# Held full-row stores, 512-column weight loads, a later place for the state products and a split last eviction in a fused linear-attention and gated-FFN kernel

## The chip, the cores and the metric

The kernel runs on one core of a Trainium2 chip. The metric is the device time of an execution in microseconds (us); on one core that is the time of that core. Each ratio compares the runs of two kernels that ran in the same rounds.

## The reference

Attention with a decaying state over blocks of the sequence, then a gated feed-forward over all tokens:

```python
# q, k, v: (4, 8, 768, 64) float32; lam: (8,); state kv: (64 x 64) per batch and head
intra = (q_b k_b^T * Dmask) v_b                  # within a block of the sequence
inter = (q_b * lam_pow) kv                       # with the state of the earlier blocks
out_b = intra + inter
kv = lam_block * kv + (k_b * rev_pow)^T v_b      # "state product"
# the 4 x 768 = 3072 tokens of 512 features:
y = (sigmoid(x @ w_gate) * (x @ w_val)) @ w_out  # 512 -> 1536 -> 512
```

## The kernel before

The kernel takes the sequence in six blocks of 128 positions (512 tokens with the batch of 4). A block has an attention part, a gate/value phase of twelve tiles (`gv`), and a projection of four token tiles (`po`). A plan lists the units, and the attention of the next block is hung behind units of this one. The order of instructions on each engine is the order of the program.

```python
def load_gv(f0, f1):                       # f0, f1: tiles of 128 columns, f32 -> bf16 on the way
    fs = slice(f0 * 128, f1 * 128)
    nc.gpsimd.dma_start(out=WG[:, :, fs], in_=wg_r[:, :, fs])
    nc.gpsimd.dma_start(out=WV[:, :, fs], in_=wv_r[:, :, fs])

def piece_po(n, tt, c0, c1, eng):          # projection of block n, token tile tt, columns c0 to c1
    ...                                    # 12 matmuls po += HT[n, ft]^T WO[:, ft, c0:c1]
    (eng.copy if eng is nc.scalar else eng.tensor_copy)(o, po[:, :c1 - c0])
    nc.sync.dma_start(out=out[..., c0:c1], in_=o)

# loads, in order, all on the gpsimd queue (cut: k, q, v of block 0; gv 0 to 6)
load_gv(6, 8)
load_gv(8, 10)
load(1, "k", 0, 2)
load(1, "q", 0, 2)
load_gv(10, 12)
load_wo(0, 256)                            # first half of WO's columns
load(1, "k", 2, 4)
load(1, "q", 2, 4)
load_wo(256, 512)                          # second half
load(1, "v")
load(2, "kq")

# block 0 (cut)
behind[5] = [pair(piece_c, 0, 0), pair(piece_c, 0, 1)]   # state products of block 0
behind[8] = [trans(1, 0)]                                # block 1: transposes, scores, masks
behind[9] = [pair(piece_s, 1, 0), m_(1, 0)]
behind[10] = [m_(1, 1)]
for ft in range(NFT):
    gv(0, ft, *behind[ft])
after = {(0, 1): [kd(1, 0)], (0, 2): [trans(1, 1)],
         (0, 3): [pair(piece_s, 1, 1), m_(1, 2), kd(1, 2)], ...}
for j in range(2):                                       # block 0's projection in two halves of
    for tt in range(B):                                  # columns, as WO's second half lands late
        po(0, tt, *after.get((j, tt), []), c=(256 * j, 256 * (j + 1)))
```

From block 2 on, k and q are transposed by DMA on the sync queue, which also issues the stores.

Of the kernel before, what the change touches and what calls it, by code (L numbers as in the profile page):

```python
# [16 lines left out]
def kernel(  # L17
# [11 lines left out]
    nc = tc.nc  # L29

    B, H, S, D = q.shape
    C = 128
    NSTEP = S // C
    HP = H // 2
    DM = H * D
# [35 lines left out]
    def swapped(n, b):  # L71
        return n > 0 and b >= NB2
# [10 lines left out]
    def load(n, what, b0=0, b1=B):  # L83
        sl = slice(n * C, (n + 1) * C)
        for c in what:
            if (c, n) not in T_:
                T_[c, n] = qkv.tile([128, B, H, D], BF16, tag=c + "b", name=c + "b",
                                      bufs=5 if c == "v" else 4)
            src = {"q": q, "k": k, "v": v}[c]
            nat = b1 if n == 0 or c == "v" else min(b1, NB2)  # L90
            if b0 < nat:
                nc.gpsimd.dma_start(  # L92
                    out=T_[c, n][:, b0:nat],
                    in_=src[b0:nat, :, sl, :].rearrange("b h s d -> s (b h) d"))
            if nat < b1:
                m = max(nat, b0)
                for u in range(2):
                    nc.gpsimd.dma_start(  # L98
                        out=T_[c, n][:, m:b1, u::2, :],
                        in_=src[m:b1, 1 - u::2, sl, :].rearrange("b h s d -> s (b h) d"))  # L100

    def load_gv(f0, f1):
# [4 lines that stand above are left out]
    def load_wo(c0, c1):  # L107
        nc.gpsimd.dma_start(out=WO[:, :, c0:c1], in_=wo_r[:, :, c0:c1])
# [110 lines left out]
    def t_(c, n, bs):  # L219
        ps = ps_at.tile([128, len(bs), HP, C], BF16, name="t" + c, tag="ps")  # L220
        for i, b in enumerate(bs):
            for hp in range(HP):
                nc.tensor.transpose(ps[:, i, hp, :], T_[c, n][:, b, 2 * hp:2 * hp + 2, :], ident)
        (tqs if c == "q" else tks)[n, bs[0]] = ps
# [15 lines left out]
    def e_k(n, bs, parts=1):  # L240
        t = trsb.tile([128, 2, HP, C], BF16, tag="KS", name="KS")
        w = len(bs) // parts
        for i in range(parts):
            nc.scalar.copy(t[:, i * w:(i + 1) * w], tks[n, bs[0]][:, i * w:(i + 1) * w])
        for i in range(len(bs)):
            KS[n, bs[i]] = t[:, i]
# [4 lines left out]
    def xbar(n):  # L251
        for c, d in (("k", KT), ("q", QT)):
            d[n] = qtp.tile([128, B, HP, C], BF16, tag=c + "t", name=c + "t")
            nc.sync.dma_start_transpose(
                out=d[n].rearrange("p b hp s -> p (b hp) s"),
                in_=T_[c, n].rearrange("p b h d -> p (b h d)"))
        for b in range(B):
            KS[n, b] = KT[n][:, b]

    def piece_s(n, bs):  # L260
        for b in bs:
            sp = [ps_at.tile([128, HP, C], FP32, name=f"sp{u}", tag="ps") for u in range(2)]
            for hp in range(HP):
                for u in range(2):
                    us = slice(u * 64, (u + 1) * 64)
                    nc.tensor.matmul(sp[u][:, hp, :], lhsT=KS[n, b][us, hp, :],  # L266
                                     rhs=QS[n, b][us, hp, :],
                                     start=(hp == 0), stop=(hp == HP - 1), skip_group_check=True)
            SP[n, b] = sp

    def piece_m(n, b):
        MT[n, b] = mtp.tile([128, 2, HP, C], BF16, tag="MT", name="MT")
        for u in range(2):
            nc.vector.tensor_tensor(out=MT[n, b][:, u], in0=SP[n, b][u],  # L274
                                    in1=(mask if n else mask0)[:, 1 - u if swapped(n, b) else u],
                                    op=ALU.mult)
# [69 lines left out]

    OB = {}

    def piece_po(n, tt, c0, c1, eng):
        if (n, tt) not in OB:  # L350
            OB[n, tt] = osb.tile([128, DM], FP32, tag="ob", name="ob")
        po = ps_ff.tile([128, DM], FP32, name="po", tag="ff")
        for ft in range(NFT):
            nc.tensor.matmul(po[:, :c1 - c0], lhsT=HT[n, ft][:, tt * 128:(tt + 1) * 128],  # L354
                             rhs=WO[:, ft, c0:c1], start=(ft == 0), stop=(ft == NFT - 1))
        o = OB[n, tt][:, c0:c1]
        (eng.copy if eng is nc.scalar else eng.tensor_copy)(o, po[:, :c1 - c0])  # L357
        nc.sync.dma_start(out=out[tt * S + n * C:tt * S + (n + 1) * C, c0:c1], in_=o)



# [2 lines left out]
    def zeros(m):  # L364
        for _ in range(m):
            nc.tensor.matmul(zps, lhsT=Sb[:, 0, 0:2, :], rhs=Sb[:, 0:2], start=True, stop=True)  # L366
# [17 lines left out]
    tables_late()  # L384
    piece_s(0, [0])
    piece_m(0, 0)
    piece_s(0, [1])
    piece_m(0, 1)
    t_("k", 0, [2, 3])
    e_k(0, [2, 3], parts=2)  # L390
    zeros(2)
    t_("q", 0, [2])
    e_q(0, [2], nc.scalar)
# [27 lines left out]
    for n in range(2):  # L421
        make_kd(n)
    load_gv(6, 8)
    load_gv(8, 10)
    load(1, "k", 0, 2)
    load(1, "q", 0, 2)
    load_gv(10, 12)
    load_wo(0, 256)
    load(1, "k", 2, 4)
    load(1, "q", 2, 4)  # L430
# [6 lines left out]
    def gate(n):  # L437
        for i, t in enumerate((KT[n], QT[n])):
            nc.gpsimd.tensor_copy(gates[:, i:i + 1], t[:, B - 1, HP - 1, C - 1:C])  # L439

    def next_loads(n):
        xbar(n)
        gate(n)
        load(n, "v")
        if n + 1 < NSTEP:
            load(n + 1, "kq")
# [5 lines left out]
    def unit(f, *more):  # L452
        plan.append((f, list(more)))

    def gv(n, ft, *more):
        unit(lambda: piece_gv(n, ft), *more)

    def po(n, tt, *more, c=(0, DM), eng=nc.scalar):
        unit(lambda: piece_po(n, tt, *c, eng), *more)

    def pair(f, n, bp):
        return lambda: f(n, [2 * bp, 2 * bp + 1])

    def m_(n, b):
        return lambda: piece_m(n, b)

    def trans(n, bp):
        def go():
            bs = [2 * bp, 2 * bp + 1]
            t_("k", n, bs)  # L470
            e_k(n, bs)
            t_("q", n, bs)
            e_q(n, bs)
        return go

    def att(n):
        def go():
            piece_i(n)
            piece_a(n, range(B))
            piece_x(n, range(B))  # L480
            if n < NSTEP - 1:
                piece_c(n, [0, 1])
                piece_c(n, [2, 3])
        return go

    def kd(n, h0):
        return lambda: piece_kd(n, [h0, h0 + 1])

    behind = {ft: [] for ft in range(NFT)}
# [2 lines left out]
    behind[0].append(swap_halves)  # L492
    behind[1].append(lambda: make_mask(0))
    behind[3].append(lambda: make_mask(1))
    behind[5] = [pair(piece_c, 0, 0), pair(piece_c, 0, 1)]
    behind[8] = [trans(1, 0)]
    behind[9] = [pair(piece_s, 1, 0), m_(1, 0)]
    behind[10] = [m_(1, 1)]
    for ft in range(NFT):
        gv(0, ft, *behind[ft])  # L500
    after = {(0, 1): [kd(1, 0)], (0, 2): [trans(1, 1)], (0, 3): [pair(piece_s, 1, 1), m_(1, 2), kd(1, 2)],
             (1, 0): [m_(1, 3), kd(1, 4)], (1, 1): [kd(1, 6)], (1, 2): [att(1)]}
    for j in range(2):
        for tt in range(B):
            po(0, tt, *after.get((j, tt), []), c=(256 * j, 256 * (j + 1)))
# [1 line left out]
    for n in range(1, NSTEP):  # L507
        nx = n + 1
        more = [[] for i in range(NFT)]
        if nx < NSTEP:  # L510
            more[3] = [lambda nx=nx: e_q(nx, [0, 1])]
            more[4] = [pair(piece_s, nx, 0), m_(nx, 0)]
            more[5] = [m_(nx, 1), lambda nx=nx: e_q(nx, [2, 3])]
            more[7] = [pair(piece_s, nx, 1), m_(nx, 2)]
            more[8] = [m_(nx, 3)]
            more[11] = [att(nx)]
        if nx < NSTEP - 1:
            for i in range(4):
                more[6 + i].append(kd(nx, 2 * i))
            more[5].append(lambda nx=nx: make_kd(nx))  # L520
        if n == 1:
            more[4:11] = more[3:10]
            more[3] = []
            more[2].append(lambda: next_loads(2))
            more[8].append(lambda: next_loads(3))
        for ft in range(NFT):
            gv(n, ft, *more[ft])
        for tt in range(B):
            if n == NSTEP - 1 and tt == B - 1:
                po(n, tt, c=(0, 256))  # L530
                po(n, tt, c=(256, 512), eng=nc.vector)
            else:
                more = [lambda n=n: next_loads(n + 3)] if tt == B - 1 and n + 3 < NSTEP else []
                po(n, tt, *more)
# [35 lines left out]
```

## Time and profile before

Median 229.34 us of 3 runs (229.26 to 229.42).

| what | value | where it is read |
|---|---|---|
| PE busy | 216.2 of 227.6 us, 95% | page |
| DMA engines busy | 90% or more in slices 1 to 10 | page, row DMA |
| PE waits for WO's second half | 1.48 us | PE waits, timeline |
| block to block, PE | 34.6 us | chain |
| last eviction's end to the end of the span | 2.89 us | timeline, last DMA |

In the views, PE is the engine of the matmuls and PEld its weight loads; ACT (scalar) and DVE (vector) copy PE's finished results out, which is called an eviction; POOL (gpsimd) issues the loads, and SPq are instructions of the sync engine, which issues the stores. WG, WV and WO are the gate, value and output weights. On PE, `zps` is a clear at the start, `tk` and `tq` are transposes of k and q, `sp` scores, `cp` state products, `gp` and `vp` the gate/value phase, and `po` the projection. KS is the copy of the transposed k that the scores read.

The page of the kernel before, the busy rows of PE and DMA (tenths, in 40 slices of 5.7 us):

```profile
span 227.6 us, 4227 instructions
PE 216.2 (95%) x1689; PEld 110.9 (49%) x1713; DVE 101.6 (45%) x186; ACT 100.9 (44%) x216; POOL 59.5 (26%) x75
...
PE   6689999979999999999999999999999999999994
...
DMA  7999999999939999995995939012100012100022
```

PE is the bound, but slice 8 of its row (counted from zero; 45.5 to 51.2 us) is not full, and the DMA engines are at least 90% busy until about 62 us, where slice 11 begins. The table of who PE waited for (total us, times, longest):

```profile
PE zps L366 <- DVE Sb L147: 1.5, 1, 1.5
PE po L354 <- DMA WO<-in_moe_w_out_dram: 1.5, 1, 1.5
PE tq L223 <- DMA qb<-in_q_dram: 1.2, 2, 0.7
```

The timeline of PE before (start, length, operation, count; in brackets the idle time ahead of it) shows where the WO wait stands: between block 1's scores (sp) and the second half of the projection (po).

```profile
44.13 1.47 PE L354 MATMUL po<-WO,ht 128*128 128x256 bf16 x12
45.54 0.62 PE L266 MATMUL sp<-QS,KS 64*128 64x128 bf16 x16
47.63 1.58 PE L354 MATMUL po<-WO,ht 128*128 128x256 bf16 x13 [1.48 <-DMA WO<-in_moe_w_out_dram]
```

While WO's second half is on its way, four stores are issued. The DMA view from 40 to 48 us, of the kernel before, gives them 12.3% of the engines' time (q1 carries sync's DMAs; q0, which queues ahead, sums overlapping packets and so passes 100%):

```profile
q0 software_dynamic: 5371, 1.27, 167.5%
q1 hardware_dynamic: 288, 0.26, 12.3%
```

The end of the kernel before: the last 256 columns are evicted by DVE, then stored. The timeline, and the record of the last store alone with its time from issue to landing:

```profile
224.25 0.42 DVE L357 COPY ob<-po 128x256 f32<-128x256 f32 x1 [9.63 <-PE po L354]
```

```profile
L358 SPq DMA_DIRECT2D out_dram<-ob x1: 332/332/332, 224.7 to 224.7; - x1
...
DMA to landing us min/median/max: 1.7/1.7/1.7
```

The eviction ends at 224.68, the store lands at 226.40, and the span ends at 227.57 us.

### The profile page before, as it was taken

The page shows a single profiled execution, that of the slowest core. Times are in us where ns is not written, and L with a number is a line of the kernel's source. Part 1 is how long each engine was busy: PE and PEld are TensorE (multiplying, and loading weights), DVE is VectorE, ACT ScalarE, POOL GpSimd, SP SyncE. Part 2 cuts the span into 40 slices and gives each one's busy share as a digit, 9 for nine tenths or more (in the row PEclk, how much of TensorE's full clock was granted, in tenths as well). Part 3 has the DMA queues.
Part 4 walks back from the last instruction along what each step waited for, and adds up shares of the span by engine and source line. Part 5 has one row for each costly group of instructions (what it writes and reads, how often), then busy time and mean ns, then how long its engine had stood idle before and what let it go on. Part 6 is the DMA issues. An engine that isn't in the chain of part 4 may idle for free.

```text
span 227.6 us, 4227 instructions
## 1 busy us (share of the span) xinstructions
PE 216.2 (95%) x1689; PEld 110.9 (49%) x1713; DVE 101.6 (45%) x186; ACT 100.9 (44%) x216; POOL 59.5 (26%) x75
## 2 busy tenths in 40 slices
PE   6689999979999999999999999999999999999994
PEld 1444454867444644444544444554444544444443
DVE  4754657145468620388430378530368600333300
ACT  5767443565337732338532328532333342333221
POOL 7997654700067009302900030000000000000000
PEclk9999999999999999999999999999999999999998
DMA  7999999999939999995995939012100012100022
GB/s 115 147 174 200 193 180 181 194 193 178 212 57 153 147 209 106 207 193 98 109 157 154 192 53 82 0 49 92 46 3 0 0 49 92 46 0 3 0 94 92
DMA packets 106195, 25.31 MB, mean 111 GB/s; under 512 B 94144, under 2 KB 103744, under 8 KB 106176
## 3 DMA queue, kind: packets, MB, share of 16 engines
q0 software_dynamic: 82816, 13.90, 79.3%
q1 hardware_dynamic: 22896, 11.01, 19.5%
q8 instruction: 13, 0.21, 0.4%
q10 hardware_dynamic: 464, 0.14, 0.3%
q14 instruction: 6, 0.05, 0.1%
HBM read 28.32 MB, written 6.29 MB: 152 GB/s over the span
## 4 chain that ended last, share of the span: by engine, by line
PE 77%; DMA 15%; POOL 5%; issue 2%; DVE 0%; POOLq 0%
PE po L354 25%; PE vp L342 23%; PE gp L336 22%; DMA WO<-in_moe_w_out_dram 7%; DMA qb<-in_q_dram 5%; DMA WG<-in_moe_w_gate_dram 3%; PE op L296 2%; PE sp L266 2%; PE op L285 1%; POOL vb L92 1%; POOL kb L92 1%; PE cp L314 1%; POOL WG L104 1%; POOL qb L92 1%; POOL WV L105 1%
## 5 line engine op out<-in xcount | busy, mean ns | idle before, releaser
L345 DVE TENSOR_TENSOR ht<-sg,vp 128x512 bf16<-128x512 bf16 x72 | 49.4, 686 | 94.3 <-PE vp L342 92.7
L342 PE MATMUL vp<-XT,WV 128*128 128x512 bf16 x287 | 73.8, 379 | 0.3
L336 PE MATMUL gp<-XT,WG 128*128 128x512 bf16 x272 | 71.5, 379 | 1.5 <-issue 0.8
L339 ACT ACTIVATE sg<-gp 128x512 bf16<-128x512 f32 x72 | 43.0, 597 | 66.5 <-PE gp L336 63.0
L354 PE MATMUL po<-WO,ht 128*128 128x512 bf16 (+1 forms) x343 | 63.6, 342 | 1.8 <-DMA WO<-in_moe_w_out_dram 1.5
L354 PEld LDWEIGHTS <-ht 128*128 128x128 bf16 x348 | 33.5, 98 | 29.8 <-issue 1.5
L342 PEld LDWEIGHTS <-WV 128*128 128x128 bf16 x288 | 28.2, 98 | 34.0 <-DMA WV<-in_moe_w_val_dram 0.2
L336 PEld LDWEIGHTS <-WG 128*128 128x128 bf16 x288 | 27.3, 98 | 32.4 <-issue 0.3
L357 ACT COPY ob<-po 128x512 f32<-128x512 f32 (+1 forms) x28 | 14.4, 515 | 45.3 <-PE po L354 45.3
L274 DVE TENSOR_TENSOR MT<-sp,mask 128x512 bf16<-128x512 f32 x48 | 30.5, 682 | 1.9 <-PE sp L266 1.9
L120 ACT ACTIVATE kd<-kb,kds 128x128 bf16<-128x128 bf16 (+1 forms) x72 | 23.8, 402 | 0.0
L439 POOL COPY gates<-kt 128x1 bf16<-128x1 bf16 x4 | 0.7, 186 | 54.8 <-DMA kt<-kb 54.8
L306 ACT CAST XT<-op 128x512 bf16<-128x512 f32 x21 | 10.9, 597 | 5.6 <-PE op L296 5.6
L92 POOL DMA_DIRECT2D vb<-in_v_dram x7 | 10.9, 1563 | 1.4 <-issue 0.9
L323 DVE SCALAR_TENSOR_TENSOR Sb<-Sb,dec,cp 128x128 bf16<-128x128 bf16 x32 | 8.6, 342 | 3.3 <-PE cp L314 3.3
L98 POOL DMA_DIRECT2D kb<-in_k_dram x10 | 8.8, 895 | 3.2 <-DMA WO<-in_moe_w_out_dram 2.3
L98 POOL DMA_DIRECT2D qb<-in_q_dram x10 | 8.9, 918 | 1.3 <-DMA kb<-in_k_dram 0.8
L92 POOL DMA_DIRECT2D qb<-in_q_dram x7 | 8.4, 1205 | 0.8 <-POOLq L554 0.8
L366 PE MATMUL zps<-Sb 128*128 128x512 bf16 x19 | 6.5, 469 | 1.6 <-DVE Sb L147 1.5
L92 POOL DMA_DIRECT2D kb<-in_k_dram x6 | 6.9, 1158 | 1.4 <-DMA WV<-in_moe_w_val_dram 0.8
L296 PE MATMUL op<-MT,vb 128*64 128x128 bf16 x184 | 6.5, 221 | 0.0
L296 PEld LDWEIGHTS <-vb 128*64 128x64 bf16 x184 | 5.3, 110 | 1.3 <-issue 0.4
(55 smaller groups left out, 81.9 us busy)
## 6 DMA issues: line engine op xcount, KB each, us to landing
out_dram<-ob SPq DMA_DIRECT2D x19, 256.0 KB, 2.0
vb<-in_v_dram POOLq DMA_DIRECT2D x5, 512.0 KB, 7.0
qb<-in_q_dram POOLq DMA_DIRECT2D x7, 256.0 KB, 8.3
kb<-in_k_dram POOLq DMA_DIRECT2D x6, 256.0 KB, 8.0
WO<-in_moe_w_out_dram POOLq DMA_DIRECT2D x2, 768.0 KB, 14.6
WG<-in_moe_w_gate_dram POOLq DMA_DIRECT2D x5, 256.0 KB, 9.2
WV<-in_moe_w_val_dram POOLq DMA_DIRECT2D x5, 256.0 KB, 9.8
kb<-in_k_dram POOLq DMA_DIRECT2D x10, 128.0 KB, 8.6
```

Of the source, the lines that this page charges most:

```text
L92: nc.gpsimd.dma_start(out=T_[c, n][:, b0:nat], in_=src[b0:nat, :, sl, :].rearrange("b h s d -> s (b h) d"))
L98: nc.gpsimd.dma_start(out=T_[c, n][:, m:b1, u::2, :], in_=src[m:b1, 1 - u::2, sl, :].rearrange("b h s d -> s (b h) d"))
L120: nc.scalar.mul(KD[n][:, at, i, :], T_["k", n][:, at, i, :], kds[:, h:h + 1])
L274: nc.vector.tensor_tensor(out=MT[n, b][:, u], in0=SP[n, b][u], in1=(mask if n else mask0)[:, 1 - u if swapped(n, b) else u], op=ALU.mult)
L296: nc.tensor.matmul(OP[n, b][rows_of(w), hp, :], lhsT=T_["v", n][:, b, h, :], rhs=MT[n, b][:, slot(n, b, h) % 2, hp, :], start=(n == 0 and ...
L306: (e.tensor_copy if e is nc.vector else e.copy)(XT[n][:, :, b, :], OP[n, b])
L336: nc.tensor.matmul(gp, lhsT=WG[:, mt, fs], rhs=x[:, mt, :], start=(mt == 0), stop=(mt == NMT - 1))
L339: nc.scalar.activation(sg, gp, AF.Sigmoid)
L342: nc.tensor.matmul(vp, lhsT=WV[:, mt, fs], rhs=x[:, mt, :], start=(mt == 0), stop=(mt == NMT - 1))
L345: nc.vector.tensor_mul(HT[n, ft], sg, vp)
L354: nc.tensor.matmul(po[:, :c1 - c0], lhsT=HT[n, ft][:, tt * 128:(tt + 1) * 128], rhs=WO[:, ft, c0:c1], start=(ft == 0), stop=(ft == NFT - 1))
L357: (eng.copy if eng is nc.scalar else eng.tensor_copy)(o, po[:, :c1 - c0])
```

## The change

Its intent is to take block 0's eight half-row stores out of the stretch in which the DMA engines are full, and to move four full-row stores into the hole near 62 us; to load the last gate/value weights in wider rows; to keep the state products off the gate/value phase; and to shorten the last eviction and store.

```diff
+    def store(n, tt, c0=0, c1=DM): ...
@@ piece_po
-        nc.sync.dma_start(out=out[...], in_=o)
+        if n:
+            store(n, tt, c0, c1)
@@ block 0's attention
     piece_s(0, [0]); piece_m(0, 0)
+    t_("k", 0, [2, 3]); e_k(0, [2, 3], parts=2)     # were after the next line
     piece_s(0, [1]); piece_m(0, 1)
@@ loads
-    load_gv(8, 10)
+    load_gv(8, 12)
     load(1, "k", 0, 2)
     load(1, "q", 0, 2)
-    load_gv(10, 12)
@@ plan of block 0
-    behind[5] = [pair(piece_c, 0, 0), pair(piece_c, 0, 1)]
-    behind[8] = [trans(1, 0)]
-    behind[9] = [pair(piece_s, 1, 0), m_(1, 0)]
-    behind[10] = [m_(1, 1)]
+    behind[10] = [trans(1, 0)]
+    behind[11] = [pair(piece_s, 1, 0), m_(1, 0)]
-    after = {(0, 1): [kd(1, 0)], (0, 2): [trans(1, 1)], ...}
+    after = {(0, 0): [m_(1, 1)], (0, 1): [kd(1, 0), trans(1, 1)],
+             (0, 2): [pair(piece_s, 1, 1), m_(1, 2), kd(1, 2)],
+             (0, 3): [pair(piece_c, 0, 0), pair(piece_c, 0, 1), m_(1, 3)], ...}
@@ block 1, tile 2 issues block 2's transposes
+            more[3].extend([lambda tt=tt: store(0, tt) for tt in range(B)])
@@ last block, last token tile
                 po(n, tt, c=(0, 256))
-                po(n, tt, c=(256, 512), eng=nc.vector)
+                po(n, tt, c=(256, 384), eng=nc.vector)
+                po(n, tt, c=(384, 512))
```

More of the change, by code (lines that the diff above doesn't have):

```diff
@@ L347, with store @@
     OB = {}
+    def store(n, tt, c0=0, c1=DM):
+        nc.sync.dma_start(out=out[tt * S + n * C:tt * S + (n + 1) * C, c0:c1],
+                          in_=OB[n, tt][:, c0:c1])
     def piece_po(n, tt, c0, c1, eng):
@@ L357, in piece_po @@
         (eng.copy if eng is nc.scalar else eng.tensor_copy)(o, po[:, :c1 - c0])
-        nc.sync.dma_start(out=out[tt * S + n * C:tt * S + (n + 1) * C, c0:c1], in_=o)
+        if n:
+            store(n, tt, c0, c1)
     zps = ps_ff.tile([128, DM], FP32, name="zps", tag="ff")
@@ L386 @@
     piece_m(0, 0)
+    t_("k", 0, [2, 3])
+    e_k(0, [2, 3], parts=2)
     piece_s(0, [1])
     piece_m(0, 1)
-    t_("k", 0, [2, 3])
-    e_k(0, [2, 3], parts=2)
     zeros(2)
@@ L494 @@
     behind[3].append(lambda: make_mask(1))
-    behind[5] = [pair(piece_c, 0, 0), pair(piece_c, 0, 1)]
-    behind[8] = [trans(1, 0)]
-    behind[9] = [pair(piece_s, 1, 0), m_(1, 0)]
-    behind[10] = [m_(1, 1)]
+    behind[10] = [trans(1, 0)]
+    behind[11] = [pair(piece_s, 1, 0), m_(1, 0)]
     for ft in range(NFT):
         gv(0, ft, *behind[ft])
-    after = {(0, 1): [kd(1, 0)], (0, 2): [trans(1, 1)], (0, 3): [pair(piece_s, 1, 1), m_(1, 2), kd(1, 2)],
-             (1, 0): [m_(1, 3), kd(1, 4)], (1, 1): [kd(1, 6)], (1, 2): [att(1)]}
+    after = {(0, 0): [m_(1, 1)], (0, 1): [kd(1, 0), trans(1, 1)],
+             (0, 2): [pair(piece_s, 1, 1), m_(1, 2), kd(1, 2)],
+             (0, 3): [pair(piece_c, 0, 0), pair(piece_c, 0, 1), m_(1, 3)],
+             (1, 0): [kd(1, 4)], (1, 1): [kd(1, 6)], (1, 2): [att(1)]}
     for j in range(2):
```

## The prediction

> **What bounds the kernel now.** PE. The page gives PE 216.2 of 227.6 us busy (95%); the chain of waits is unbroken PE work from 47.6 us on, about 34.6 us a block. The table of PE waits lists 1.5 us for the clear at the start, 1.5 us for the second half of WO (projection 0's second half starts at 47.63), and 0.7 us or less each. A second limit lies beneath the first 62 us: the page's DMA row reads 9 in slices 1 to 10; weights and q, k, v land back to back in issue order. The change can win only the WO wait, start gaps, and the tail.
>
> **Terms, from landings and durations in the trace.**
>
> 1. Stores. Before, 128 KB stores are issued at 41.2, 42.5, 44.0, 46.0 us, beside the second WO load, which landed 4.9 us after its predecessor (42.67 to 47.59). The Trainium skill, "DMA: Bandwidth & Descriptors", "Queues, rings and completion order", says each engine alternates between queues at packet granularity; I estimate the load alone at 4.0 us (three times the 1.33 us that a third of its bytes took). Holding the stores: WO lands 0.9 us earlier. They go out near 60 us, where the DMA row falls to 3.
> 2. 512-column weights. Landing intervals are 0.73 us for 128 columns, 1.33 for 256, by extrapolation 2.53 for 512: 0.25 us saved over both tensors. Price: WV for tiles 8 to 11 lands whole, at 26.0 + 2 x 2.53 = 31.1 us, and PE, without the state products in its gate/value phase, wants it at 30.8: a NEW wait of 0.3 us at tile 8. k and q of block 1 land about 34.5 to 35.6; PE wants them at 35.5 to 35.9 (transposes moved to tile 10): just in time.
> 3. State products (0.6 us) only move. Projection 0's first half starts at about 39.0 in both, bound by the first WO half.
> 4. ScalarE order: transposes now follow the second token tile, behind four decay products (1.27 us) and an eviction; the KS copy (1.0 us) ends about 2.7 us after that tile, while PE wants it after 2.3 (0.9 transposes + 1.37 tile). NEW wait of 0.4 us at block 1's scores.
>
> PE then reaches the second half at 47.0, WO having landed at 46.4: the WO wait is gone, but replaced in part. Gain 0.6 us instead of 1.5.
>
> 5. Transposes ahead of stores on the sync queue: the first, issued at 56.17, comes at about 53; PE did not wait there. No gain.
> 6. Start: moving the k transposes up fills a 0.5 us gap, but the next q transpose still waits for q, landing at 11.12. No gain.
> 7. Tail: last eviction 128x256 on DVE (0.42 us) becomes 128x128 on ACT (estimate 0.26); the last store halves (landing 1.37 us, estimate 0.1 less). 24 matmuls of 128 columns at 56 ns (the transposes' pace) equal 12 of 256 at 114. Gain 0.25 us.
>
> **Sum:** 0.6 + 0.25 = 0.85 us: 228.5 us, 8 in 10 between 227.6 and 229.2. Faster by over 2%: 0.01; within 2%: 0.98; slower: 0.01.
>
> **Right if the profile shows:** no PE wait on WO's second half; small new waits on WV at tile 8 and on KS at scores; first transpose before 55 us; the DMA hole near 62 us filled by stores; blocks 2 to 5 unchanged at 34.6 us.
>
> **Wrong if:** WV or q land later (gain lost), ScalarE has slack I missed (gain up to 2 us), or late stores delay the next transposes enough to stall PE.

## The result

The changed kernel took 229.35 us (median of 4 runs, 229.03 to 229.65) against 229.31 us: ratio 1.0001, 95% interval 0.9983 to 1.0018. There is no gain, and the time lies above my range of 227.6 to 229.2. Ratios here and below are the mean time of one kernel's runs over that of the kernel before in the same rounds, so not quite the ratio of the medians quoted. Executions over 1.5% slower than the fastest of the same kernel are left out of the means. A difference in us between two kernels below is the difference of their ratios times 229.3 us; where the two ran in different calls it rests on the kernel before, which ran in each.

The page of the changed kernel, the rows shown before:

```profile
span 227.2 us, 4266 instructions
PE 218.9 (96%) x1725; PEld 111.2 (49%) x1725; DVE 101.8 (45%) x186; ACT 101.2 (45%) x217; POOL 58.1 (26%) x73
...
PE   6789999999999999999999999999999999999993
...
DMA  7999999999999929993992959012100012100022
```

PE's row has lost the dent at slice 8. (The two busy times of PE don't compare: the kernel before has 1689 records of PE in this trace, and some are missing: held stores alone, below, has the same matmuls and 1713 records.) The hole of the DMA row at slice 11 (counted from zero, 62.5 to 68.2 us) is gone: the held stores go out from 59.1 us, and the loads behind them start 3.4 us earlier than before, so that the next hole comes at slice 14. PE's waits after:

```profile
PE zps L371 <- DVE Sb L147: 1.5, 1, 1.5
...
PE vp L342 <- DMA WV<-in_moe_w_val_dram: 0.3, 1, 0.3
```

The WO wait is gone, and a wait on WV of 0.33 us is new. The timeline of PE after, at the same place; the state products (cp) now stand ahead of the second half:

```profile
43.98 0.62 PE L266 MATMUL sp<-QS,KS 64*128 64x128 bf16 x16
44.53 1.49 PE L358 MATMUL po<-WO,ht 128*128 128x256 bf16 x12
45.95 0.69 PE L314 MATMUL cp<-vb,kd 128*64 128x64 bf16 x32
46.57 2.68 PE L358 MATMUL po<-WO,ht 128*128 128x256 bf16 x23
```

The second half starts at 46.57 instead of 47.63, 1.06 us earlier, and nothing is lost on the way to the last projection: it starts at 212.69 instead of 213.66, so 166.12 us later against 166.03 before. The last eviction is shorter too and ends at 223.58 instead of 224.68: 1.10 us ahead. But the span ends only 0.40 us earlier. The end of the changed kernel, its timeline and the record of the last store:

```profile
222.64 0.29 DVE L361 COPY ob<-po 128x128 f32<-128x128 f32 x1 [8.99 <-PE po L358]
223.31 0.27 ACT L361 COPY ob<-po 128x128 f32<-128x128 f32 x1 [0.97 <-PE po L358]
```

```profile
L350 SPq DMA_DIRECT2D out_dram<-ob x1: 333/333/333, 223.8 to 223.8; - x1
...
DMA to landing us min/median/max: 2.0/2.0/2.0
```

The store with half the bytes took 2.0 us from its issue, not 1.7; and it was issued 0.24 us after its eviction ended, not 0.03. So PE's microsecond was real in this trace, and 0.70 us of it went after PE had finished. (This trace is of the fastest of the four runs. About 0.25 us of its lead was luck at the start: the gate/value phase began at 15.85 us, against 16.08 in the kernel before and 16.11 in the repeat below, as q landed at 10.89 us, against 11.12 and 11.15. The rest of the difference to the average is within the spread of the runs.) The question is why the end of the kernel became longer.

### The profile page after: what moved, and what is told of

It is laid out like the page before. It is cut to its first block, busy times and chain, and to the rows that moved or that the text cites. A ratio compares the mean times of both kernels' runs of the same rounds, so it can differ in the third digit from the quotient of the medians.

```text
span 227.2 us, 4266 instructions
## 1 busy us (share of the span) xinstructions
PE 218.9 (96%) x1725; PEld 111.2 (49%) x1725; DVE 101.8 (45%) x186; ACT 101.2 (45%) x217; POOL 58.1 (26%) x73
## 4 chain that ended last, share of the span: by engine, by line
PE 84%; DMA 9%; POOL 4%; ACT 1%; issue 1%; POOLq 0%
PE po L358 27%; PE vp L342 24%; PE gp L336 24%; DMA WV<-in_moe_w_val_dram 6%; DMA vb<-in_v_dram 3%; PE sp L266 2%; PE op L296 2%; PE op L285 1%; PE cp L314 1%; POOL WV L105 1%; POOL WG L104 1%; POOL qb L92 1%; POOL vb L92 1%; ACT kd L120 1%; POOL kb L92 0%
## 5 line engine op out<-in xcount | busy, mean ns | idle before, releaser
L336 PE MATMUL gp<-XT,WG 128*128 128x512 bf16 x288 | 74.0, 379 | 0.4 <-ACT XT L421 0.4
L358 PE MATMUL po<-WO,ht 128*128 128x512 bf16 (+2 forms) x360 | 64.1, 337 | 0.0
L361 ACT COPY ob<-po 128x512 f32<-128x512 f32 (+2 forms) x29 | 14.7, 507 | 46.4 <-PE po L358 46.4
L443 POOL COPY gates<-kt 128x1 bf16<-128x1 bf16 x4 | 1.2, 304 | 52.1 <-DMA kt<-kb 52.1
L371 PE MATMUL zps<-Sb 128*128 128x512 bf16 x21 | 7.5, 482 | 1.5 <-DVE Sb L147 1.5
```

What stands on the lines that cost most here:

```text
L336: nc.tensor.matmul(gp, lhsT=WG[:, mt, fs], rhs=x[:, mt, :], start=(mt == 0), stop=(mt == NMT - 1))
L358: nc.tensor.matmul(po[:, :c1 - c0], lhsT=HT[n, ft][:, tt * 128:(tt + 1) * 128], rhs=WO[:, ft, c0:c1], start=(ft == 0), stop=(ft == NFT - 1))
```

## The experiments

Two marks are used throughout: the start of projection 0's second half on PE ("second half"), and the tail, in two pieces: from the end of the last eviction to the landing of the last store, and from there to the end of the span. The first runs are numbered 1, those of the second and third call 2 and 3; each call shared one chip and its runs of the kernel before.

| kernel | median us | ratio to before, 95% | second half | eviction to landing | landing to end |
|---|---|---|---|---|---|
| before (first trace) | 229.34 | | 47.63 | 1.73 | 1.16 |
| changed | 229.35 | 1.0001 (0.9983 to 1.0018) | 46.57 | 2.24 | 1.35 |
| 1 changed, again | 229.23 | 1.0001 (0.9989 to 1.0013) | 46.78 | 2.23 | 1.33 |
| 1 changed, old tail | 228.56 | 0.9969 (0.9957 to 0.9981) | 46.9 | 1.82 | 0.91 |
| 1 before, new tail | 228.93 | 0.9984 (0.9972 to 0.9996) | 47.50 | 1.58 | 1.08 |
| 1 changed, one last store | 228.49 | 0.9970 (0.9958 to 0.9982) | 47.0 | 1.74 | 0.93 |
| 2 changed, 8 stores cut | 229.06 | 0.9986 (0.9974 to 0.9999) | 47.3 | 1.58 | 1.33 |
| 2 changed, 7 stores cut | 228.47 | 0.9961 (0.9948 to 0.9973) | 47.2 | 1.69 | 0.91 |
| 2 before, held stores | 228.19 | 0.9955 (0.9943 to 0.9967) | 46.62 | 1.84 | 0.91 |
| 2 held stores, new tail | 228.96 | 0.9982 (0.9968 to 0.9995) | 46.33 | 2.27 | 1.35 |
| 3 changed, held as halves | 228.56 | 0.9968 (0.9954 to 0.9981) | 46.7 | 1.58 | 1.10 |
| 3 held, new tail, 7 cut | 227.56 | 0.9931 (0.9919 to 0.9944) | 46.24 | 1.63 | 0.90 |
| 3 changed, 2 x 256, old tail | 228.75 | 0.9976 (0.9963 to 0.9988) | 47.1 | 1.83 | 0.91 |
| 3 changed, loads as before, old tail | 228.86 | 0.9978 (0.9965 to 0.9990) | 47.32 | 1.80 | 0.91 |

The column "second half" comes from one trace each and moves by 0.2 us or more between two traces of the same kernel (46.57 and 46.78), as the landings of the loads do. The two columns of the tail repeat to 0.02 us in the repeated kernel, so they can be read finely. Every run of the experiments gave a correct result.

### First call: is the tail at fault?

**The changed kernel again**, without an edit.

> The changed kernel once more, for its spread and a second trace. In the first trace PE starts projection 0's second half at 46.57 us (before: 47.63) and the last eviction ends 1.09 us earlier, but the last store lands only 0.58 us earlier. Theory (tail): about 0.5 us of the gain is always lost after the last eviction; expect again 2.2 us from the end of the last eviction to the landing of the last store, against 1.7 in the kernel before. Rival (jitter): that 0.5 us was an accident of one trace and the missing gain lies in start or DMA jitter; expect about 1.7 us there. Time: 229.0 to 229.7 us in both.

The long tail is no accident: 2.23 us again.

**The changed kernel with the old tail.**

```diff
-                po(n, tt, c=(256, 384), eng=nc.vector)
-                po(n, tt, c=(384, 512))
+                po(n, tt, c=(256, 512), eng=nc.vector)
```

> The changed kernel with the last token tile's stores as before (256 + 256 columns, the last eviction on DVE). Theory (tail): PE gain stays at about 1 us and the tail returns to 1.7 us: faster than the changed kernel by 0.3 to 0.5 us, about 228.8 us. Rival (jitter, or gain lost elsewhere): same time as the changed kernel within 0.15 us.

0.71 us faster than the kernel before: the new tail takes all of what the rest gains.

**The kernel before with the new tail**, the same edit the other way round.

> The kernel before with only the new tail (256 + 128 + 128 columns). Theory (tail): slower than before by 0.3 to 0.5 us, about 229.7 us, with the last store landing 2.2 us after the last eviction. Rival, my prediction's tail term: 0.25 us faster, about 229.05 us.

My theory in its first form fell here. The same tail made the kernel before 0.37 us *faster*, with a last store that landed 1.58 us after its eviction, 0.14 us quicker than with the old tail. By the traces of the two kernels, 0.16 us come from the shorter eviction, 0.14 from the landing and 0.08 from what follows it. So the split tail is good by itself, as predicted, and bad in the changed kernel. The record of the last store in this run:

```profile
L358 SPq DMA_DIRECT2D out_dram<-ob x1: 333/333/333, 224.7 to 224.7; - x1
...
DMA to landing us min/median/max: 1.6/1.6/1.6
```

**The changed kernel with one store for both last pieces.**

```diff
-        if n:
+        if n == NSTEP - 1 and tt == B - 1 and c0 >= 256:
+            if c1 == DM:
+                store(n, tt, 256, 512)
+        elif n:
             store(n, tt, c0, c1)
```

> The changed kernel with the last 128 + 128 columns evicted as in the change, but stored by one DMA of 256 columns after both. If the extra store on the sync queue (its issue directly behind another, or its 512-byte rows) is what costs the 0.5 us, the store lands about 1.7 us after the eviction's end and the time falls by 0.4 to 0.6 us against the changed kernel, to about 228.75 us, and 0.1 to 0.2 us under the old tail. If the loss comes from the short eviction or from the 128-column matmuls, the time stays within 0.15 us of the changed kernel.

The long tail goes, and the kernel is 0.71 us faster than the changed one, as expected of "the extra store costs it", but after the run before this one that reading is not enough: the extra store costs nothing in the kernel before.

The records of the sync engine tell the two apart. Below are its last instructions in the changed kernel, then in the kernel before with the new tail, as I list them from the trace: number of the record from zero (the expectations call record 79 the 79th), start, idle time since the instruction before it, what it is.

```
changed kernel
 77  222.747   0.045  semaphore wait
 78  222.960   0.196  store, columns 256 to 384
 79  223.738   0.446  semaphore wait (semaphore 107, long since reached)
 80  223.817   0.062  store, columns 384 to 512
 81  224.202   0.052  closing waits begin; 107 is met at 225.836, then seven more of 0.06 us each

kernel before, new tail
 78  217.170  22.913  store, first token tile of the last block
 79  217.949   0.447  semaphore wait (semaphore 107, long since reached)
 ...
 87  224.416   0.046  semaphore wait
 88  224.680   0.247  store, columns 384 to 512
 89  225.058   0.045  closing waits begin; 115 is met at 226.256, then three more
```

In both, record 79 starts after a pause of 0.45 us in which nothing it waits for is missing. About 0.6 to 0.85 us after it, one packet of 8192 bytes runs on queue 14. The Trainium skill, "CRC Debugging", "Comparing the Two Runs", names queue 14 as that of the sequencers' instruction refill; "Runtime: NRT & Kernel Launch", "Instruction fetch mechanics", says that a sequencer fetches its next instructions through a DMA queue while it executes, at a cost that is "one DMA tail-bump, mostly hidden". In the kernel before with the new tail the pause is hidden, at 217.95 us, with a wait of 1.8 us behind it. The changed kernel issues four stores for block 0 instead of eight and has eight sync records fewer, so its record 79 is the one just ahead of the last store. There the packet seems to do further harm. The DMA view of the changed kernel after 223.7 us has both queues at work; in the kernel before, after 224.6 us, there is q1 alone:

```profile
q1 hardware_dynamic: 289, 0.13, 10.5%
q14 instruction: 1, 0.01, 0.9%
```

```profile
q1 hardware_dynamic: 152, 0.13, 11.7%
```

In the packet records of the changed kernel the refill runs from 224.38 to 225.00 us, and a last group of eight 512-byte packets of the store starts at 225.00 and ends at 225.19, when all the others are done by 224.99. Eight packets are one engine's share, if the 128 rows are spread evenly over the 16 DMA engines. The landing followed at 225.82. The updates of the store's semaphore tell the same: 16 come, fifteen of them by 225.52 us and the last at 225.82, 0.30 us later. In the repeat of the changed kernel the last is 0.26 us late, and in one more kernel with the long tail (held stores with the new tail, below) 0.30 us; in the other eleven traces it is never more than 0.05 us behind. So of the 0.66 us by which eviction to landing is longer than in the kernel before with the new tail, 0.22 is the later issue, 0.15 the first fifteen updates and 0.29 the sixteenth. That the refill holds up the one share is inferred from the times, as the trace does not say on which DMA engine a packet ran.

A third piece is the list of closing waits, in the fixed order 107, 109, 111, 114, 115, 116, 117, 118, with 0.06 us a wait. The last store of the changed kernel has semaphore 107, so seven waits come after its landing; with 118 there are none. The ends of 1.16 us with semaphore 114 (the kernel before) and 1.08 us with 115 fit this: four and three waits more than the 0.91 us with 118.

### Second call: move the count of sync instructions, and nothing else

**The changed kernel with eight, and with seven, of its later stores cut in two** (same bytes, in blocks 3 and 4, where the DMA row of the page reads 0 to 2).

```diff
-        if n:
+        if n in (3, 4) and 4 * (n - 3) + tt < 8:     # or < 7
+            store(n, tt, 0, 256)
+            store(n, tt, 256, 512)
+        elif n:
             store(n, tt, c0, c1)
```

> The changed kernel with all eight stores of blocks 3 and 4 cut into two of 256 columns, same bytes. In every trace so far the sync engine pauses 0.45 us before its 79th recorded instruction, and an 8 KB packet of the instruction queue follows about 1 us later; in the changed kernel, which issues fewer stores, the 79th is the one just before the last store. Theory (instruction fetch): 16 more instructions earlier move the pause away from the tail, the last store lands about 1.6 us after the last eviction instead of 2.2, and since the last store keeps its semaphore, the end after the landing stays 1.33 us. About 0.65 us faster than the changed kernel: 228.6 us. Rival (128-column stores back to back cost it): tail stays 2.2 us, 229.2 us.

> The same with seven stores cut. The pause is away from the tail too, but the last store's semaphore is now the last in the sync engine's closing list (118 instead of 107). Theory (list order): the tail after the landing shrinks from 1.33 to about 0.93 us, as the old-tail and one-store runs had it with 118; 0.3 to 0.4 us faster than split8, about 228.2 us. Rival: the order of the list is of no account, same time as split8 within 0.15 us.

More stores, and the tail is shorter. With eight cut, record 79 with its pause is at 217.56 us, the refill packet runs at 218.37, and the last store lands 1.58 us after its eviction. Its record:

```profile
L350 SPq DMA_DIRECT2D out_dram<-ob x1: 332/332/332, 224.3 to 224.3; - x1
...
DMA to landing us min/median/max: 1.6/1.6/1.6
```

The end after the landing is still 1.33 us, with semaphore 107 as before. With seven cut, the last store has semaphore 118 and the end is 0.91 us; that kernel was 0.57 us faster than the one with eight cut, where I expected 0.3 to 0.4; the tails of the two traces (2.60 and 2.91 us) account for 0.31 of it. (No pause shows among its records; the refill packet is at 218.24, so the pause would lie inside a 2.2 us wait.) The eight-cut kernel's time was a disappointment: 0.32 us under the kernel before, where 0.65 was expected. Its tail is 0.65 us shorter by the trace, but in that trace WV landed at 31.72 instead of 31.01 to 31.22 us and PE began the second half 0.5 us later than in the repeat of the changed kernel; its edit touches nothing that early. The loads do spread as much: in seven traces of kernels that are alike up to there, WV landed at 31.01 to 31.72 us. That this spread hid the gain in the average of the five runs is argued, not shown.

**The kernel before with held stores alone**: the `store` function, `if n:`, and the four held stores of the change's diff, nothing else.

> The kernel before with block 0's stores held as full rows, nothing else. Theory: WO's second half lands about 0.9 to 1.4 us earlier, the WO wait of 1.4 us shrinks below 0.5, and as no new wait arises on WV the gain at projection 0's second half is about 1 us. The pause of the sync engine falls after the last issue here. Time 228.1 to 228.5 us. Rival (DMA is not slowed by the stores): wait on WO stays above 1 us, time within 0.4 us of before.

1.03 us faster than the kernel before: this one piece of the change is worth more than the whole. (About 0.15 us of it lies at the end: with the last store on semaphore 118 the two pieces of the tail take 2.74 us, against 2.89.) WO's second half landed at 46.58 instead of 47.59 us, and PE's wait fell to 0.42:

```profile
46.62 4.09 PE L358 MATMUL po<-WO,ht 128*128 128x256 bf16 x36 [0.42 <-DMA WO<-in_moe_w_out_dram]
```

The DMA view of this kernel from 40 to 48 us has no row for q1 any more, and q0 gets through more:

```profile
q0 software_dynamic: 6453, 1.41, 194.8%
q14 instruction: 2, 0.02, 0.5%
```

With the old tail, record 79 falls after the last store's issue, where it waits for the landing anyway, and the semaphore is 118.

**Held stores and the new tail.**

> Held stores and the new tail, without the rest. Theory (instruction fetch): the 79th sync instruction is again the one before the last store, so the tail costs 2.2 us, and this is 0.5 to 0.8 us SLOWER than held stores with the old tail, although the same tail made the kernel before 0.35 us faster. Rival: the tail gains 0.3 us here too.

0.62 us slower than held stores alone: the tail that gained 0.37 us in the kernel before loses here, because record 79 (at 223.41, after a pause of 0.446) is again the one ahead of the last store, and 2.27 + 1.35 us follow the eviction. Here too a group of eight packets of the store starts only as the refill packet ends, at 224.69.

### Third call: the rest of the change, and the best of both

**The changed kernel with the held stores as eight halves.**

```diff
-            more[3].extend([lambda tt=tt: store(0, tt) for tt in range(B)])
+            more[3].extend([lambda tt=tt, c0=c0: store(0, tt, c0, c0 + 256)
+                            for c0 in (0, 256) for tt in range(B)])
```

> The changed kernel with block 0's output still held, but stored as eight halves instead of four full rows. Theory (count of sync instructions): eight more sync instructions than the changed kernel put the 0.45 us pause back to where the kernel before had it, the last store lands about 1.6 us after the last eviction, and its semaphore is 115, in mid-list, so about 1.1 us follow: 0.7 to 0.9 us faster than the changed kernel, 228.4 to 228.6 us. Rival (full rows are the cheaper stores and that is what matters): same as or slower than the changed kernel, 229.2 us or more.

0.73 us faster than the kernel before, and 0.76 than the changed one. The full rows, which look like the cheaper stores, brought the loss, by the trace through the number of instructions: pause at 216.94 us, tail 1.58 + 1.10.

**Held stores, new tail, seven later stores cut**, loads and order as before.

> Held stores, new tail, and seven later stores cut in two, so that the pause is away and the last semaphore is last in the list; loads and order as before. Theory: eviction to landing 1.6 us, landing to end 0.91 us, last eviction 0.15 us shorter: about 0.2 us under held stores with the old tail, 228.0 us, the fastest of all. Rival: no better than held stores alone within 0.1 us, as the shorter eviction is paid back by the two stores back to back.

227.56 us, 1.58 us faster than the kernel before, and the fastest of all. From the start of the last eviction to the end of the span it takes 2.79 us, against 3.17 with held stores alone; that explains 0.38 of the 0.55 us between the two. The rest is in the trace as WO landing 0.38 us earlier, which the edit does not explain. The record of its last store:

```profile
L350 SPq DMA_DIRECT2D out_dram<-ob x1: 333/333/333, 223.2 to 223.2; - x1
...
DMA to landing us min/median/max: 1.6/1.6/1.6
```

**The changed kernel, old tail, the last weights in 2 x 256 columns** in the same place of the order (`load_gv(8, 10); load_gv(10, 12)` for `load_gv(8, 12)`).

> The changed kernel with the old tail and its last weights in 2 x 256 columns, in the same place of the order. Theory: 512 columns cost the wait on WV at tile 8 (0.3 to 0.4 us), nothing else; it goes, and PE reaches projection 0's second half 0.3 us earlier unless WO's second half (46.2 to 46.4 us) then makes it wait: 0.1 to 0.3 us faster than the 512 columns with the old tail, about 228.3 to 228.45 us. Rival: the wait merely moves to q or WO, same time.

The rival held. The wait on WV at tile 8 went, but waits on WO's first half (0.46 us) and on q (0.37 us) took its place, and the time is that of the 512 columns within the intervals (ratios 0.9976 and 0.9969). No gain or loss from the width of these rows is clear of the noise.

**The changed kernel, old tail, loads in the order of before.** Against held stores alone only the order of the work differs.

> Held stores, old tail, loads as before, but the order of the change (k transposes up, state products in projection 0, block 1's transposes at tile 10). Apart from held stores alone only the order differs. Theory: the order gains nothing, since the work before projection 0's second half is the same and WO's landing bounds it: within 0.15 us of held stores alone, 228.2 us; KS may wait 0.2 us at block 1's scores, hidden under the WO wait of 0.4 us. Rival: the order is worth up to 0.4 us, 227.8 us.

My expectation was wrong. The order did not gain nothing, it lost: 0.53 us slower than held stores alone (ratios 0.9978 and 0.9955). The timeline of PE in this run:

```profile
32.80 1.03 PE L342 MATMUL vp<-XT,WV 128*128 128x512 bf16 x4
33.88 1.04 PE L336 MATMUL gp<-XT,WG 128*128 128x512 bf16 x4
35.26 1.04 PE L342 MATMUL vp<-XT,WV 128*128 128x512 bf16 x4 [0.33 <-DMA WV<-in_moe_w_val_dram]
...
42.03 0.61 PE L223 MATMUL tk<-ident,kb 128*128 128x128 bf16 x8
42.73 0.61 PE L223 MATMUL tq<-ident,qb 128*128 128x128 bf16 x8
...
46.69 0.69 PE L314 MATMUL cp<-vb,kd 128*64 128x64 bf16 x32
47.32 4.10 PE L358 MATMUL po<-WO,ht 128*128 128x256 bf16 x36
```

Four vp or gp matmuls take 0.86 us from start to start. Here the steps are 1.08 and 1.38 us at 32.80 and 33.88, so PE lost 0.22 + 0.52 us to weights landing at 33 to 35 us, since the state products, transposes and scores that used to stand in the gate/value phase no longer fill the time until they land. From tk to tq it is 0.70 us where it should be 0.45, for q. The work was all needed before the second half, and there it can no longer hide a wait. PE found WO ready at 47.32 us, 0.8 us after it had landed (46.53).

## Why the prediction was wrong

The sum failed by one term, and the rest of it came close.

- **What bounds the kernel: right.** PE, with the WO wait as the one thing to win outside the ends. The blocks are unchanged to 0.1 us over five of them.
- **Term 1, the stores: right.** "WO lands 0.9 us earlier": with held stores alone it landed 1.01 us earlier, and the time fell by 1.03 us, about 0.15 of it at the end of the span.
- **Term 2, 512 columns: right.** The 512 columns of the two tensors took 2.54 and 2.55 us (2.53 predicted), WV landed at 31.01 us (31.1), PE waited 0.33 us for it (0.3).
- **Terms 3 and 4, the order: right in kind.** The wait on KS was nothing in the first trace and 0.21 us in the second, not 0.4; a wait of about 0.25 us for q at block 1's second transposes, which I did not list, came beside it. PE reached the second half at 46.57 and 46.78 us; I had 47.0. The new waits together cost about 0.3 us (ratio 0.9969 with the old tail against 0.9955 for held stores alone). All of the change but its tail gained 0.71 us, for the 0.6 of terms 1 to 4, and 0.16 of the 0.71 lies at the end (2.73 against 2.89 us).
- **Terms 5 and 6: right.** The first DMA transpose was issued at 52.67 us, for "about 53"; the gate/value phase started at 15.85 and 16.11 us, against 16.08.
- **Term 7, the tail: wrong, and this is the step that failed.** I wrote "Gain 0.25 us", from the shorter eviction and the smaller store. Alone, on the kernel before, that tail gained 0.37 us: eviction and landing as forecast (0.16 and 0.14 us, for 0.16 and 0.1), and 0.08 us by the luck of a later place in the closing list. In the changed kernel it cost 0.73 us: old tail 0.9969, new tail 1.0001. I had costed the tail as if its pieces did not depend on what came before. But the change elsewhere removed eight records of the sync engine, and this moved a 0.45 us pause and an 8 KB packet, which were hidden before, to just before the last store, and gave that store the first semaphore of the closing list in place of a middle one. Three runs that change only the number of earlier stores (eight cut, seven cut, halves) took the pause away from the tail, and with it the 2.2 us landing. Of the 0.70 us that the first trace lost after the last eviction, 0.52 lie before the landing and 0.19 after it.

What stays open is small: that the pause and the packet are the sequencer fetching instructions rests on the queue and on its moving with the count, not on a record that says so. Pause and packet came together wherever the pause shows, so what each of them costs is read from the pieces of the trace and not from a run that has one without the other.

The version to keep is held stores with the new tail and a count of sync instructions that keeps the pause off the end: 227.56 us, against 229.3 for both kernels.

## What to carry to other kernels

When a change moves PE's finish and not the time, read the end of the span on the issuing engine instruction by instruction: what follows the last matmul is pure critical path. A change that alters how many instructions an engine issues can move fixed pauses of that engine, so test a tail on the very program that it ends; here one edit was worth a gain of 0.37 us on one program and a loss of 0.73 us on another. And filler work on PE is best left where loads are late: moved behind them it fills nothing.

## What the Trainium skill lacked or had wrong

- "Runtime: NRT & Kernel Launch", "Instruction fetch mechanics", calls the crossing of a block of instructions "mostly hidden". Here the pause that I take for it is 0.45 us on the sync engine, 0.44 to 0.46 in all traces that show it, and in front of the last store it was not hidden: with the packet's collision it cost about 0.65 us from eviction to landing (2.24 against 1.58). The page also gives blocks of 16 KiB; what followed each pause on queue 14 was a single packet of 8192 bytes, so no run here shows such a block.
- No page that I read tells what a refill packet costs a store that it meets, though "DMA: Bandwidth & Descriptors", "Queues, rings and completion order", lists the refill among the queues that share the DMA engines. Here the last eight 512-byte packets started at 225.00 us as the refill ended, with the others done by 224.99, and the last of the 16 semaphore updates came 0.26 to 0.30 us late in the three traces with the long tail.
- No page that I read tells what the closing waits cost: 0.06 us for each semaphore after the last store's, so 1.33 to 1.35 us from landing to the end with the first of eight and 0.90 to 0.93 with the last.
- "DMA: Bandwidth & Descriptors", "Queues, rings and completion order", on engines alternating between queues, is in keeping with the runs as far as they go: without the stores beside it WO landed 1.01 us earlier (47.59 and 46.58). That they alternate by packet no run here shows.
